# Gate and value weights by expert outputs: side by side fp32 products and a group sum in place of split products

## Chip, cores and metric

The kernel runs on one core of one Trainium2 chip. Its time is the device time of one execution in microseconds (us), and the median of several executions is what counts. Five engines work beside each other, each through its own instructions in order: TensorE (PE, with its weight loads listed apart as PEld), VectorE (DVE), ScalarE (ACT), GpSimd (POOL), and SyncE (SP), which issues the transfers.

## What is computed

Three layers follow one another; all inputs come as float64 and the output is float32.

```python
# chunked attention, 64 tokens a chunk, 8 heads of 64
attn = softmax(scale * q_c @ k_c.T); x = attn @ v_c            # x: 4608 x 512
# soft mixture of experts, 8 experts of 4 slots
logits = x @ phi                                               # 4608 x 32
slot_input = softmax(logits, axis=0).T @ x                     # 32 x 512
slot_out[e] = relu(slot_input[e] @ w1[e]) @ w2[e]              # 32 x 512
x2 = softmax(logits, axis=1) @ slot_out                        # 4608 x 512
# gated layer
g = x2 @ w_gate; val = x2 @ w_val                              # 512 -> 1536
out = (g * sigmoid(g) * val) @ w_out                           # 1536 -> 512
```

Since x2 has rank 32, the kernel never forms it. With C the 4608 x 32 matrix of combine weights, g = C @ (slot_out @ w_gate), and the same for val. The change lies in the small inner product slot_out @ w_gate and slot_out @ w_val.

## The kernel before

**Stages.** Attention, logits and slot inputs run until about 130 us, the experts until about 170 us, and the gated layer from there to the end. The rest concerns the gated layer.

**Chunks.** The 1536 inner columns come as six chunks `c` of 256 (`NSC`), so twelve tiles `f` of 128. Chunk 0 has a path of its own. For a chunk `c` of 1 to 5 the weights w_gate, w_val and w_out arrive as float64 words and are turned into float32 in halves `u` of 1024 words, in four steps over four turns of the main loop: `conv_a` (L174) takes the words apart on ACT and DVE, `conv_b` (L194) goes on with them, `conv_c` (L202) makes the exponent on DVE (L203) and multiplies on POOL (L216), and `conv_d` (L231) splits the float32 value into a high part, rounded to the short fp32r format by ACT (L237), and the rest, by POOL or DVE in turn (L242). High part and rest go into a tile `whl`. The queue `conv_q` goes through gate half 0, gate half 1, value 0, value 1, out 0, out 1 of each chunk; how far it is, `conv_pos()` (L262) counts.

**Inner product.** `emit_g` (L825) multiplies `so_hl` (slot_out transposed, in four blocks `kk` of 128 rows, its high part three times over and its rest once, in 128 columns) by the split weights: for gate and for value four blocks and two parts each, so 16 matmuls of 256 columns into the PSUM tile `gg_ps`. `evac_g` (L812) then copies them to `g_st` on ACT and replaces one group of 32 partitions by its rest on DVE. `try_g` (L958), at the end of a turn, calls it once the four gate and value halves have been through all four steps.

**Main loop** (L973). There are 108 pairs of a block `b` of 512 tokens and a tile `f`, in an order given by `SCHED`. Turn `n` issues in this order: `emit_gv` (L843), two matmuls `g_ps` and `v_ps`, then silu on ACT (L853) and the product `s_sb` on DVE (L854); `emit_hl` for the pair before (L870), its high part on ACT (L860) and its rest `lo_sb` on POOL (L867); one `conv_step`; `emit_out` (L877) for the pair two turns back, 12 matmuls of 512 columns (L894), and, when a group of pairs ends, the addition of four tiles of output to `part` (L912); and `try_g`. So each engine sees the turns in this order, and PE has 14 matmuls a turn beside the inner product.

**Buffers.** PSUM has three buffers for `g_ps`, `v_ps` and the inner product (`ps_g`). Weights, words and splits share 16 buffers (`wp`), which `freed` and `pump` hand on to the next transfer.

Of the kernel before, what the change touches and what calls it, by code (L numbers as in the profile page):

```python
# [8 lines left out]
F32 = mybir.dt.float32  # L9
F32R = mybir.dt.float32r  # L10
# [4 lines left out]
ACTF = mybir.ActivationFunctionType  # L15
ALU = mybir.AluOpType
# [18 lines left out]
def tile_attn_softmoe_swiglu(  # L35
# [12 lines left out]
    nc = tc.nc  # L48
# [6 lines left out]
    NSC = w_gate.shape[0]  # L55
# [10 lines left out]
    sel_big = const.tile([128, 4, 32], F32, name="sel_big")  # L66
# [10 lines left out]
    raw_t = {}  # L77
# [39 lines left out]

    hl_t = {}

    def alloc_hl(kind, c, pool):  # L120
        hl_t[kind, c] = wp.tile([128, 2048], F32R, tag="w", name="whl")

# [3 lines left out]
        tmp_t.append(pool.tile([128, 2048], I32, tag="w", name="tmp"))  # L126

    def sc_loads(c, kinds="gvo"):
        return [(f, kd, c) for kd in kinds for f in (load_raw, alloc_hl)]

    lq = [(load_gv0, 0), (alloc_tmp, 0)]
    EG = 4
# [27 lines left out]
    def freed(f, *a):  # L160
        slots[owner.pop((f.__name__, a))] += 1
        if auto[0]:
            pump()
# [37 lines left out]
    def conv_c():  # L201
        kind, c, u, hh, ex, m = stage["c"].pop(0)  # L202
        nc.vector.scalar_tensor_tensor(out=ex, in0=hh, scalar=0x8000, in1=ex,  # L203
                                       op0=ALU.bitwise_and, op1=ALU.bitwise_or)
        p = ex.bitcast(BF16)
        if c == 0 and kind != "o":
            nc.gpsimd.tensor_tensor(
                out=w_f32(u)[:, :, "gv".index(kind), :], in0=m.rearrange("p (k f) -> p k f", k=4),
                in1=p.rearrange("p (k f) -> p k f", k=4), op=ALU.mult,
            )  # L210
            if kind == "v":
                if u == 0:
                    freed(load_gv0, 0)
                freed(alloc_tmp, u)
            return
        nc.gpsimd.tensor_tensor(out=m, in0=m, in1=p, op=ALU.mult)  # L216
        stage["d"].append((kind, c, u, m))
        if u == 1:
            freed(load_raw, kind, c)
# [3 lines left out]
            return wf0  # L223
        return raw0[0, ff].bitcast(F32).rearrange("p (k a f) -> p k a f", a=2, f=128)

    def w_split(kind, c):
        return hl_t[kind, c].rearrange("p (k h f) -> p k h f", h=2, f=512 if kind == "o" else 256)

    n_d = [0]

    def conv_d(eng=None, hi_eng=None):  # L231
        kind, c, u, m = stage["d"].pop(0)
        k = 1 if kind == "o" else 2
        w = w_split(kind, c)[:, k * u:k * (u + 1)]
        m = m.rearrange("p (k f) -> p k f", k=k)
        if hi_eng is None:
            nc.scalar.activation(out=w[:, :, 0], in_=m, func=ACTF.Copy)  # L237
        else:
            hi_eng.tensor_copy(out=w[:, :, 0], in_=m)
        eng = eng or (nc.vector if n_d[0] % 2 else nc.gpsimd)  # L240
        n_d[0] += 1
        eng.tensor_tensor(out=w[:, :, 1], in0=m, in1=w[:, :, 0].bitcast(F32), op=ALU.subtract)  # L242

    def conv_ready():
        if not conv_q:
            return False
        kd, c, u = conv_q[-1]
        if c == 0 and kd != "o":
            return ("gv".index(kd), u) in raw0
        return (kd, c) in raw_t and (kd, c) in hl_t  # L250

    def conv_step(start=True, which="dcba"):
        for k, f in (("d", conv_d), ("c", conv_c), ("b", conv_b)):
# [8 lines left out]
    def conv_pos():  # L262
        n = len(conv_q) + sum(len(x) for x in stage.values())
        return 6 * NSC - n
# [6 lines left out]
    with tc.manual_schedule():  # L271
# [32 lines left out]
        for i in range(NV):  # L304
            nc.vector.memset(v_bd[i][0:64, 1], 0.0)
        nc.vector.tensor_reduce(
            out=sel_big[:, 0, :], in_=ident.rearrange("p (j s) -> p s j", s=32), axis=AX.X, op=ALU.add
        )
        nc.vector.tensor_tensor(
            out=sel_h.rearrange("p a s -> p (a s)"), in0=ident[:, 0:64], in1=ident[:, 64:128], op=ALU.add  # L310
# [237 lines left out]
        for k in range(NP + 1):  # L548
            a = k - 1
# [251 lines left out]
        ps_g = ctx.enter_context(tc.tile_pool(name="ps_g", bufs=3, space=PSUM, reuse_waits="tile"))  # L801
        ht2 = ctx.enter_context(tc.tile_pool(name="ht2", bufs=3, side="right"))
        g_st = ht2.tile([128, NSC, 2, 256], F32R, name="g_st", bufs=1)
        so_hl = ht2.tile([128, 4, 128], F32R, name="so_hl", bufs=1)

        def emit_so_hl():
            nc.scalar.activation(out=so_hl[:, :, 0:96], in_=so_t[:, :, 0:96], func=ACTF.Copy)
            nc.vector.tensor_tensor(
                out=so_hl[:, :, 96:128], in0=so_t[:, :, 0:32], in1=so_hl[:, :, 0:32].bitcast(F32), op=ALU.subtract
            )  # L810

        def evac_g(ps, gst):  # L812
            nc.scalar.activation(out=gst, in_=ps, func=ACTF.Copy)
# [8 lines left out]
                freed(load_gv0, ff)  # L822
            return lambda: evac_g(gp, g_st[:, 0, gi, ff * 128:(ff + 1) * 128])

        def emit_g(c):  # L825
            gp = ps_g.tile([128, 2, 256], F32, tag="g", name="gg_ps")
            for gi in range(2):
                w = w_split("gv"[gi], c)
                for kk in range(4):
                    for h in range(2):  # L830
                        nc.tensor.matmul(out=gp[:, gi], lhsT=so_hl[:, kk, :], rhs=w[:, kk, h],  # L831
                                         start=(kk == 0 and h == 0), stop=(kk == 3 and h == 1))
            evac_g(gp, g_st[:, c])
            freed(alloc_hl, "g", c)
            freed(alloc_hl, "v", c)

        hl = {}
        s_t = {}
# [38 lines left out]
        def emit_out(b, f, first, last, mid=None, subs=()):  # L877
            hi, lo = hl.pop((b, f))
            c, ff = f // 2, f % 2
            w = w_split("o", c)  # L880
            w_hi, w_lo = w[:, ff, 0], w[:, ff, 1]
            done = f == NFT - 1
            subs = dict(subs)
            if last and not done and b not in part:
                assert slots[0]
                slots[0] -= 1
                resv[0] -= 1
                part[b] = wp.tile([128, 4, DM], F32, tag="w", name="part"), True

            def product(t, i):  # L890
                x, w = ((hi, w_hi), (hi, w_lo), (lo, w_hi))[i]
                if first and i == 0:
                    acc_t[t] = ps_o.tile([128, DM], F32, tag="o", name=f"o{t}")
                nc.tensor.matmul(out=acc_t[t], lhsT=x[:, t * 128:(t + 1) * 128], rhs=w,  # L894
                                 start=(first and i == 0), stop=(last and i == 2))

            if mid:
                for i in range(3):
                    for t in range(4):
                        product(t, i)  # L900
                    if i == 0:
                        mid()
            for t in range(4):
                if not mid:
# [52 lines left out]

        def try_g():  # L958
            c = g_done[0]
            if c < NSC and conv_pos() >= 6 * c + 4:  # L960
                emit_g(c)
                g_done[0] += 1

        LAG = 2

# [7 lines left out]
        for n in range(1, len(seq) + LAG):  # L973
            if n < len(seq):
                c = gvs[n][1] // 2
                conv_until(6 * c + 4)
                while g_done[0] <= c:
                    try_g()
            if 1 < n < len(seq):
                emit_gv(*gvs[n])  # L980
            if 3 < n <= len(seq):
                emit_hl(*gvs[n - 1], nc.gpsimd)
            m = 1 if n == 2 else n - LAG if n > 3 else None
            start = 36 - len(conv_q) < RATE * n + R0
# [12 lines left out]
            if m is not None:
                out_step(m, subs)
                try_g()
            if n == 4:  # L1000
                emit_so_hl()


_INS = ['qk', 'v', 'moe_phi', 'moe_w1', 'moe_w2', 'moe2_w_gate', 'moe2_w_val', 'moe2_w_out']
# [48 lines left out]
```

## Time and profile before

| | us |
|---|---|
| median of 3 runs | 545.22 (544.48 to 545.23) |
| the profiled execution | 543.5 |
| its span in the trace | 541.7 |
| PE busy | 521.6 (96%) |
| DVE busy | 401.2 (74%) |
| ACT busy | 260.6 (48%) |
| POOL busy | 251.2 (46%) |

The span lies between the first and the last instruction; 1.8 us of the execution lie around it. A busy PE says only that matmuls were under way: they overlap, so that what one costs is read from start to start and not from its own duration.

### The profile page before, as it was taken

How to read it: one execution, taken by the hardware profiler on the slowest of the kernel's cores; microseconds unless marked ns; L12 is line 12 of the kernel's file. 1: busy time of each engine (PE TensorE's matmuls, PEld its weight loads, DVE VectorE, ACT ScalarE, POOL GpSimd, SP SyncE). 2: the span in 40 equal slices, each digit the busy share in tenths (PEclk: the TensorE clock that was granted, in tenths of full speed). 3: DMA queues.
4: the chain of work that ended last, by engine and by line, in shares of the span. 5: the costliest groups of instructions: out<-in, count | busy, mean ns of one | idle time of the engine just before them, and what ended most of it. 6: DMA issues, size and time to landing. Idle time of an engine off the chain costs nothing.

```text
span 541.7 us, 11050 instructions
## 1 busy us (share of the span) xinstructions
PE 521.6 (96%) x4389; PEld 409.0 (76%) x4389; DVE 401.2 (74%) x681; ACT 260.6 (48%) x505; POOL 251.2 (46%) x251
## 2 busy tenths in 40 slices
PE   7899999998999789999999999999999999999997
PEld 6788877873435568888888788788878888888885
DVE  5788888764765878898899978988888863444454
ACT  1344433333446666676555546555555543333331
POOL 3244343331003276675665646674666563443342
PEclk9999999999999999999999999999999999999999
DMA  8999999999999600102200240014000000222244
GB/s 326 405 363 400 353 400 342 412 415 379 422 416 413 267 1 16 64 1 79 77 1 0 79 155 2 4 74 156 0 1 0 2 1 1 77 79 89 103 179 173
DMA packets 23906, 91.09 MB, mean 168 GB/s; under 512 B 3120, under 2 KB 3120, under 8 KB 17968
## 3 DMA queue, kind: packets, MB, share of 16 engines
q1 hardware_dynamic: 23856, 90.40, 43.2%
q8 instruction: 34, 0.56, 0.4%
q14 instruction: 16, 0.13, 0.1%
HBM read 80.95 MB, written 9.44 MB: 167 GB/s over the span
## 4 chain that ended last, share of the span: by engine, by line
PE 87%; DVE 6%; ACT 2%; issue 2%; POOL 1%; DMA 1%; SPq 0%; ACTq 0%; DVEq 0%; POOLq 0%
PE o L894 52%; PE v_ps L850 4%; PE g_ps L850 4%; PE xa_ps L368 4%; PE s_ps L331 3%; PE so_ps L698 3%; PE xt_ps L404 3%; PE h_ps L655 3%; PE pt_ps L354 3%; PE gg_ps L831 2%; PE si_ps L487 2%; DVE m L339 1%; DVE ssb L341 1%; PE lt_ps L423 1%; PE xb_ps L368 1%
## 5 line engine op out<-in xcount | busy, mean ns | idle before, releaser
L894 PE MATMUL o<-whl,hi_sb 128*128 128x512 f32 x864 | 266.9, 390 | 2.8 <-ACT whl L237 2.6
L867 POOL TENSOR_TENSOR lo_sb<-s_sb,hi_sb 128x512 fp32r<-128x512 f32 x106 | 142.4, 1344 | 129.1 <-ACT hi_sb L860 127.2
L894 PEld LDWEIGHTS o<-whl,hi_sb 128*128 128x128 f32 x864 | 161.8, 188 | 37.6 <-ACT whl L237 3.0
L894 PE MATMUL o<-whl,lo_sb 128*128 128x512 f32 x432 | 168.8, 392 | 1.7 <-POOL lo_sb L867 1.6
L853 ACT ACTIVATE s_sb<-g_ps 128x512 f32<-128x512 f32 (+1 forms) x110 | 64.5, 589 | 133.9 <-PE g_ps L850 122.5
L854 DVE TENSOR_TENSOR s_sb<-s_sb,v_ps 128x512 f32<-128x512 f32 (+1 forms) x110 | 73.9, 674 | 68.5 <-ACT s_sb L853 65.3
L894 PEld LDWEIGHTS o<-whl,lo_sb 128*128 128x128 f32 x432 | 81.1, 188 | 21.4 <-POOL lo_sb L867 4.7
L860 ACT ACTIVATE hi_sb<-s_sb 128x512 fp32r<-128x512 f32 (+1 forms) x110 | 67.7, 617 | 2.4 <-DVE s_sb L854 2.4
L912 DVE TENSOR_TENSOR part<-part,o 128x512 f32<-128x512 f32 x100 | 62.0, 678 | 2.6 <-PE o L894 2.6
L321 POOL COPY vbd<-vbd 64x520 f32<-64x520 f32 x36 | 22.6, 628 | 70.0 <-DMA vbd<-in_v_dram 54.4
L216 POOL TENSOR_TENSOR mt<-mt,ex 128x512 f32<-128x512 f32 x32 | 38.3, 1196 | 30.8 <-DVE ex L203 22.0
L203 DVE SCALAR_TENSOR_TENSOR ex<-raw,ex 128x512 uint16<-128x512 uint16 x32 | 44.0, 1374 | 0.5 <-ACT ex L197 0.5
L850 PE MATMUL v_ps<-c_t,g_st 128*128 128x512 f32 (+1 forms) x110 | 42.4, 389 | 0.7 <-ACT s_sb L853 0.6
L850 PE MATMUL g_ps<-c_t,g_st 128*128 128x512 f32 (+1 forms) x110 | 42.2, 387 | 0.1
L356 ACT ACTIVATE pt<-pt_ps 128x512 f32<-128x512 f32 x36 | 19.5, 596 | 37.4 <-PE pt_ps L354 37.4
L198 DVE SCALAR_TENSOR_TENSOR mt<-mt,raw 128x512 f32<-128x512 f32 x32 | 34.6, 1081 | 0.1
L339 DVE TENSOR_REDUCE m<-s_ps 128x16 f32<-128x1024 f32 x18 | 22.1, 1225 | 14.7 <-PE s_ps L331 14.7
L368 PE MATMUL xa_ps<-vbd,pt 128*64 128x130 f32 x432 | 28.2, 277 | 0.5 <-issue 0.5
L190 DVE TENSOR_SCALAR mt<-raw 128x512 int32<-128x512 int32 x32 | 27.2, 851 | 0.0
L237 ACT ACTIVATE whl<-mt 128x512 fp32r<-128x512 f32 x32 | 20.3, 633 | 13.4 <-POOL mt L216 13.0
L368 PEld LDWEIGHTS xa_ps<-vbd,pt 128*64 128x64 f32 x432 | 23.7, 135 | 3.2 <-issue 2.3
L406 ACT ACTIVATE xt<-xt_ps 128x512 f32<-128x512 f32 (+1 forms) x36 | 19.3, 596 | 13.3 <-PE xt_ps L404 9.7
(131 smaller groups left out, 613.4 us busy)
## 6 DMA issues: line engine op xcount, KB each, us to landing
qk<-in_qk_dram SPq DMA_DIRECT2D x36, 512.0 KB, 6.4
w1t<-in_moe_w_dram SPq DMA_DIRECT2D x16, 1024.0 KB, 9.1
w2t<-in_moe_w_dram SPq DMA_DIRECT2D x15, 1024.0 KB, 13.5
vbd<-in_v_dram SPq DMA_DIRECT2D x36, 260.0 KB, 7.4
out_dram<-part SPq DMA_DIRECT2D x36, 256.0 KB, 2.1
raw<-in_moe_w_gate_dram SPq DMA_DIRECT2D x5, 1024.0 KB, 4.8
raw<-in_moe_w_val_dram SPq DMA_DIRECT2D x5, 1024.0 KB, 4.9
raw<-in_moe_w_out_dram SPq DMA_DIRECT2D x5, 1024.0 KB, 4.8
```

Source lines behind the costliest of these rows:

```text
L198: nc.vector.scalar_tensor_tensor(out=m, in0=m, scalar=-7.0, in1=lw.bitcast(F32), op0=ALU.add, op1=ALU.add)
L203: nc.vector.scalar_tensor_tensor(out=ex, in0=hh, scalar=0x8000, in1=ex, op0=ALU.bitwise_and, op1=ALU.bitwise_or)
L216: nc.gpsimd.tensor_tensor(out=m, in0=m, in1=p, op=ALU.mult)
L339: nc.vector.tensor_reduce(out=m, in_=sv, axis=AX.X, op=ALU.max)
L368: nc.tensor.matmul(out=banks[n // 3][64 * cc:64 * cc + 64, (n % 3) * 2 * VW:(n % 3 + 1) * 2 * VW], lhsT=pt_t[i][:, j, 64 * cc:64 * cc + 64 ...
L850: nc.tensor.matmul(out=ps[:, k], lhsT=g_st[:, c, gi, ff:ff + 128], rhs=c_blk(b)[:, k], start=True, stop=True)
L853: nc.scalar.activation(out=s[:, k], in_=gp[:, k], func=ACTF.Silu)
L854: nc.vector.tensor_tensor(out=s[:, k], in0=s[:, k], in1=vp[:, k], op=ALU.mult)
L860: nc.scalar.activation(out=hi[:, k], in_=s_t[b, f][:, k], func=ACTF.Copy)
L867: eng.tensor_tensor(out=lo[:, k], in0=s[:, k], in1=hi[:, k].bitcast(F32), op=ALU.subtract)
L894: nc.tensor.matmul(out=acc_t[t], lhsT=x[:, t * 128:(t + 1) * 128], rhs=w, start=(first and i == 0), stop=(last and i == 2))
L912: nc.vector.tensor_tensor(out=p[:, t], in0=p[:, t], in1=a, op=ALU.add)
```

## The change

The gate and value weights of chunks 1 to 5 are no longer split. `conv_c` writes its product into a float32 tile `gw`, four blocks of 128 rows by gate and value by 256 columns, and these halves are done there; `conv_d` is left for w_out alone. The inner product has two parts now, in two turns. `emit_ga` multiplies four blocks in float32, each by 32 columns of `so_t`, into four groups of 32 partitions of `ga_ps`, so that the sums over the blocks are not made yet. ACT makes the high part `ghi` of the whole, and DVE the rest `glo`. At the end of the next turn `emit_gb` multiplies each of the two by `sel_r`, a matrix of zeros and ones that adds the four groups and writes the sum three times (its last 32 columns are zero), and `evac_g` follows as before. `emit_sel` makes `sel_r` in place of `so_hl`.

```diff
+    def alloc_gw(c, pool):
+        gw_t[c] = pool.tile([128, 4, 2, 256], F32, tag="w", name="gw")
...
     def sc_loads(c, kinds="gvo"):
-        return [(f, kd, c) for kd in kinds for f in (load_raw, alloc_hl)]
+        gw = [(load_raw, kd, c) for kd in "gv"] + [(alloc_gw, c)]
+        return (gw if "g" in kinds else []) + [(load_raw, "o", c), (alloc_hl, "o", c)]
...
+        if kind != "o":
+            nc.gpsimd.tensor_tensor(
+                out=gw_t[c][:, 2 * u:2 * u + 2, "gv".index(kind)], in0=m.rearrange("p (k f) -> p k f", k=2),
+                in1=p.rearrange("p (k f) -> p k f", k=2), op=ALU.mult,
+            )
+            if u == 1:
+                freed(load_raw, kind, c)
+            return
         nc.gpsimd.tensor_tensor(out=m, in0=m, in1=p, op=ALU.mult)
         stage["d"].append((kind, c, u, m))
...
-        so_hl = ht2.tile([128, 4, 128], F32R, name="so_hl", bufs=1)
-
-        def emit_so_hl():
-            nc.scalar.activation(out=so_hl[:, :, 0:96], in_=so_t[:, :, 0:96], func=ACTF.Copy)
-            nc.vector.tensor_tensor(
-                out=so_hl[:, :, 96:128], in0=so_t[:, :, 0:32], in1=so_hl[:, :, 0:32].bitcast(F32), op=ALU.subtract
-            )
+        sel_r = ht2.tile([128, 128], F32R, name="sel_r", bufs=1)
+
+        def emit_sel():
+            nc.scalar.activation(out=sel_r[:, 0:96], in_=sel_big.rearrange("p j s -> p (j s)")[:, 0:96], func=ACTF.Copy)
+            nc.scalar.activation(out=sel_r[:, 96:128], in_=so_t[:, 0, 96:128], func=ACTF.Copy)
...
-        def emit_g(c):
-            gp = ps_g.tile([128, 2, 256], F32, tag="g", name="gg_ps")
-            for gi in range(2):
-                w = w_split("gv"[gi], c)
-                for kk in range(4):
-                    for h in range(2):
-                        nc.tensor.matmul(out=gp[:, gi], lhsT=so_hl[:, kk, :], rhs=w[:, kk, h],
-                                         start=(kk == 0 and h == 0), stop=(kk == 3 and h == 1))
+        gs_t = {}
+
+        def emit_ga(c):
+            gp = ps_g.tile([128, 512], F32, tag="g", name="ga_ps")
+            w = gw_t.pop(c)
+            for kk in range(4):
+                nc.tensor.matmul(out=gp[32 * kk:32 * kk + 32, :], lhsT=so_t[:, kk, 0:32],
+                                 rhs=w[:, kk].rearrange("p a f -> p (a f)"), start=True, stop=True,
+                                 tile_position=(0, 32 * kk))
+            hi = ht2.tile([128, 512], F32R, tag="ghi", name="ghi", bufs=1)
+            nc.scalar.activation(out=hi, in_=gp, func=ACTF.Copy)
+            lo = ht2.tile([128, 512], F32R, tag="glo", name="glo", bufs=1)
+            nc.vector.tensor_tensor(out=lo, in0=gp, in1=hi.bitcast(F32), op=ALU.subtract)
+            gs_t[c] = hi, lo
+            freed(alloc_gw, c)
+
+        def emit_gb(c):
+            gp = ps_g.tile([128, 2, 256], F32, tag="g", name="gb_ps")
+            for i, x in enumerate(gs_t.pop(c)):
+                nc.tensor.matmul(out=gp.rearrange("p a f -> p (a f)"), lhsT=sel_r, rhs=x, start=(i == 0), stop=(i == 1))
             evac_g(gp, g_st[:, c])
...
         def try_g():
             c = g_done[0]
-            if c < NSC and conv_pos() >= 6 * c + 4:
-                emit_g(c)
+            if c in gs_t:
+                emit_gb(c)
                 g_done[0] += 1
+            elif c < NSC and conv_pos() >= 6 * c + 4:
+                emit_ga(c)
```

**Where the instructions stand.** On PE, at chunk 1, the inner product of before (`gg_ps`, L831) follows the 12 output products of a turn:

```order
L850 MATMUL g_ps<-c_t,g_st 128x512
L850 MATMUL v_ps<-c_t,g_st 128x512
L894 MATMUL o_3211<-whl,hi_sb 128x512 x2
L894 MATMUL o_3211<-whl,lo_sb 128x512
L894 MATMUL o_3215<-whl,hi_sb 128x512 x2
L894 MATMUL o_3215<-whl,lo_sb 128x512
L894 MATMUL o_3219<-whl,hi_sb 128x512 x2
L894 MATMUL o_3219<-whl,lo_sb 128x512
L894 MATMUL o_3223<-whl,hi_sb 128x512 x2
L894 MATMUL o_3223<-whl,lo_sb 128x512
L831 MATMUL gg_ps<-whl,so_hl 128x256 x16
L850 MATMUL g_ps<-c_t,g_st 128x512
```

With the change the same piece begins with `ga_ps`, one turn earlier, ahead of the `g_ps` that is the first row above, and ends with the first of the two products `gb_ps` at the place where `gg_ps` stood:

```order
L841 MATMUL ga_ps<-gw,so_t 32x512 x4
L870 MATMUL g_ps<-c_t,g_st 128x512
L870 MATMUL v_ps<-c_t,g_st 128x512
L914 MATMUL o_3213<-whl,hi_sb 128x512 x2
L914 MATMUL o_3213<-whl,lo_sb 128x512
L914 MATMUL o_3217<-whl,hi_sb 128x512 x2
L914 MATMUL o_3217<-whl,lo_sb 128x512
L914 MATMUL o_3221<-whl,hi_sb 128x512 x2
L914 MATMUL o_3221<-whl,lo_sb 128x512
L914 MATMUL o_3225<-whl,hi_sb 128x512 x2
L914 MATMUL o_3225<-whl,lo_sb 128x512
L854 MATMUL gb_ps<-ghi,sel_r 128x512
```

So the four fp32 products moved one turn ahead and two products of 512 columns stand where the 16 of 256 columns were; chunks 2 to 5 are alike. With their waits (what engine's signal an instruction waits for stands in brackets), the rows of `ga_ps` are these:

```order
L841 MATMUL ga_ps<-gw,so_t 32x512 [waits DVE_49]
L841 MATMUL ga_ps<-gw,so_t 32x512
L841 MATMUL ga_ps<-gw,so_t 32x512 [waits Pool_49]
L841 MATMUL ga_ps<-gw,so_t 32x512
L870 MATMUL g_ps<-c_t,g_st 128x512 [waits Activation_49]
L870 MATMUL v_ps<-c_t,g_st 128x512 [waits DVE_49]
```

The third of the four, which reads half 1 of the weights, waits for POOL, and everything after it on PE stands behind that wait.

On POOL, at chunk 1 again, a value half went through its product (`mt<-mt,ex`, L216) in one turn, and through `conv_d` (`whl`, L242) a turn later for every other half; `lo_sb` is the rest of a pair, one a turn:

```order
L867 TENSOR_TENSOR lo_sb<-s_sb,hi_sb 128x512 x3
L216 TENSOR_TENSOR mt<-mt,ex 128x512
L867 TENSOR_TENSOR lo_sb<-s_sb,hi_sb 128x512
L242 TENSOR_TENSOR whl<-mt,whl 128x2x256
L867 TENSOR_TENSOR lo_sb<-s_sb,hi_sb 128x512
L216 TENSOR_TENSOR mt<-mt,ex 128x512
L867 TENSOR_TENSOR lo_sb<-s_sb,hi_sb 128x512 x3
```

With the change the products of value half 0 and value half 1 write `gw`, and no `whl` stands between the `lo_sb`:

```order
L887 TENSOR_TENSOR lo_sb<-s_sb,hi_sb 128x512 x3
L223 TENSOR_TENSOR gw<-mt,ex 128x2x256
L887 TENSOR_TENSOR lo_sb<-s_sb,hi_sb 128x512 x2
L223 TENSOR_TENSOR gw<-mt,ex 128x2x256
L887 TENSOR_TENSOR lo_sb<-s_sb,hi_sb 128x512 x3
```

The product of value half 1 (the second `gw`) keeps its turn, and stands behind the `lo_sb` of that turn. It is the one for which the third product `ga_ps` waits.

## Rows read from the trace of the kernel before

**Rows 1.** Stretch: length, busy PE, PEld, DVE, ACT, POOL, TensorE's clock, DMA share, GB/s

```profile
203.10:529.80 326.70, 326.64 (x1470) 269.77 (x1469) 246.25 (x333) 169.19 (x299) 184.79 (x142) 1.00 0.15 52
```

**Rows 2.** Chain that ended last: inner products of chunks 1 and 3 (start, us, what)

```profile
212.75 1.91 PE gg_ps L831 x16
...
318.95 1.91 PE gg_ps L831 x16
```

**Rows 3.** Timeline of PE about chunk 5's inner product (start, us, operation)

```profile
419.03 0.39 PE L850 MATMUL g_ps<-c_t,g_st 128*128 128x512 f32 x1
...
422.21 0.39 PE L850 MATMUL g_ps<-c_t,g_st 128*128 128x512 f32 x1
...
425.39 2.34 PE L831 MATMUL gg_ps<-whl,so_hl 128*128 128x256 f32 x16
427.56 0.40 PE L850 MATMUL g_ps<-c_t,g_st 128*128 128x512 f32 x1
```

**Rows 4.** Waits of PE's weight loads, 206 to 530 us (total, times, longest)

```profile
PEld o L894 <- POOL lo_sb L867: 1.7, 5, 0.4
PEld o L894 <- DVE part L912: 0.6, 2, 0.3
PEld gg_ps L831 <- DVE whl L242: 0.4, 2, 0.2
```

**Rows 5.** Timeline of DVE and POOL in the same turn as the first row of rows 3

```profile
420.15 0.69 DVE L854 TENSOR_TENSOR s_sb<-s_sb,v_ps 128x512 f32<-128x512 f32 x1 [0.77 <-ACT s_sb L853]
...
420.71 1.29 POOL L867 TENSOR_TENSOR lo_sb<-s_sb,hi_sb 128x512 fp32r<-128x512 f32 x1 [1.89 <-ACT hi_sb L860]
420.75 1.80 DVE L203 SCALAR_TENSOR_TENSOR ex<-raw,ex 128x512 uint16<-128x512 uint16 x1
...
422.63 1.17 POOL L216 TENSOR_TENSOR mt<-mt,ex 128x512 f32<-128x512 f32 x1 [0.62 <-PE g_ps L850]
```

**Rows 6.** Timeline of the same turn in chunk 2, from its g_ps on

```profile
258.96 0.39 PE L850 MATMUL g_ps<-c_t,g_st 128*128 128x512 f32 x1
...
260.68 0.72 DVE L203 SCALAR_TENSOR_TENSOR ex<-raw,ex 128x512 uint16<-128x512 uint16 x1
...
260.82 1.75 POOL L867 TENSOR_TENSOR lo_sb<-s_sb,hi_sb 128x512 fp32r<-128x512 f32 x1
...
262.52 1.18 POOL L216 TENSOR_TENSOR mt<-mt,ex 128x512 f32<-128x512 f32 x1
```

**Rows 7.** Timeline of PE: four fp32 products side by side (x8), and what follows

```profile
126.64 1.07 PE L487 MATMUL si_ps<-x_sb,e 128*32 128x512 f32 x8
127.64 0.33 PE L469 MATMUL e_ps<-ident,et 128*128 128x128 f32 x1
...
131.48 1.92 PE L655 MATMUL h_ps<-w1t,si_m 128*32 128x512 f32 x16 [0.34 <-DVE si_m L633]
133.34 0.38 PE L755 MATMUL zps<-za,sel_big 128*128 128x1 f32 x2
```

**Rows 8.** Groups by line, 203 to 450 us (count | busy us, mean ns | idle before)

```profile
L242 POOL TENSOR_TENSOR whl<-mt,whl 128x512 fp32r<-128x512 f32 x14 | 20.2, 1445 | 0.0
L237 ACT ACTIVATE whl<-mt 128x512 fp32r<-128x512 f32 x28 | 17.7, 633 | 8.5 <-POOL mt L216 8.2
L242 DVE TENSOR_TENSOR whl<-mt,whl 128x512 fp32r<-128x512 f32 x14 | 14.5, 1039 | 6.6 <-ACT whl L237 6.6
L814 DVE TENSOR_TENSOR g_st<-gg_ps,g_st 32x512 fp32r<-32x512 f32 x5 | 3.4, 690 | 6.0 <-ACT g_st L813 6.0
```

**Rows 9.** Timeline of two early turns: PE, POOL and the waits between them

```profile
193.34 1.34 POOL L242 TENSOR_TENSOR whl<-mt,whl 128x512 fp32r<-128x512 f32 x1
...
195.83 0.39 PE L850 MATMUL g_ps<-c_t,g_st 128*128 128x512 f32 x1
...
197.10 0.50 PE L894 MATMUL o<-whl,lo_sb 128*128 128x512 f32 x1 [0.20 <-POOL lo_sb L867]
...
203.07 0.39 PE L850 MATMUL g_ps<-c_t,g_st 128*128 128x512 f32 x1
```

More of the change, by code (lines that the diff above doesn't have):

```diff
@@ L118, in tile_attn_softmoe_swiglu @@
     hl_t = {}
+    gw_t = {}
+    def alloc_gw(c, pool):
+        gw_t[c] = pool.tile([128, 4, 2, 256], F32, tag="w", name="gw")
     def alloc_hl(kind, c, pool):
@@ L224, in w_f32, with w_split @@
         return raw0[0, ff].bitcast(F32).rearrange("p (k a f) -> p k a f", a=2, f=128)
-    def w_split(kind, c):
-        return hl_t[kind, c].rearrange("p (k h f) -> p k h f", h=2, f=512 if kind == "o" else 256)
+    def w_split(c):
+        return hl_t["o", c].rearrange("p (k h f) -> p k h f", h=2, f=512)
     n_d = [0]
@@ L232, in conv_d @@
         kind, c, u, m = stage["d"].pop(0)
-        k = 1 if kind == "o" else 2
-        w = w_split(kind, c)[:, k * u:k * (u + 1)]
-        m = m.rearrange("p (k f) -> p k f", k=k)
+        w = w_split(c)[:, u]
         if hi_eng is None:
-            nc.scalar.activation(out=w[:, :, 0], in_=m, func=ACTF.Copy)
+            nc.scalar.activation(out=w[:, 0], in_=m, func=ACTF.Copy)
         else:
-            hi_eng.tensor_copy(out=w[:, :, 0], in_=m)
+            hi_eng.tensor_copy(out=w[:, 0], in_=m)
         eng = eng or (nc.vector if n_d[0] % 2 else nc.gpsimd)
         n_d[0] += 1
-        eng.tensor_tensor(out=w[:, :, 1], in0=m, in1=w[:, :, 0].bitcast(F32), op=ALU.subtract)
+        eng.tensor_tensor(out=w[:, 1], in0=m, in1=w[:, 0].bitcast(F32), op=ALU.subtract)
     def conv_ready():
@@ L249, in conv_ready @@
             return ("gv".index(kd), u) in raw0
-        return (kd, c) in raw_t and (kd, c) in hl_t
+        return (kd, c) in raw_t and ((kd, c) in hl_t if kd == "o" else c in gw_t)
     def conv_step(start=True, which="dcba"):
@@ L823, in emit_g0 @@
             return lambda: evac_g(gp, g_st[:, 0, gi, ff * 128:(ff + 1) * 128])
-        def emit_g(c):
-            gp = ps_g.tile([128, 2, 256], F32, tag="g", name="gg_ps")
-            for gi in range(2):
-                w = w_split("gv"[gi], c)
-                for kk in range(4):
-                    for h in range(2):
-                        nc.tensor.matmul(out=gp[:, gi], lhsT=so_hl[:, kk, :], rhs=w[:, kk, h],
-                                         start=(kk == 0 and h == 0), stop=(kk == 3 and h == 1))
+        gs_t = {}
[16 more added lines that the diff above has]
+                nc.tensor.matmul(out=gp.rearrange("p a f -> p (a f)"), lhsT=sel_r, rhs=x, start=(i == 0), stop=(i == 1))
             evac_g(gp, g_st[:, c])
-            freed(alloc_hl, "g", c)
-            freed(alloc_hl, "v", c)
         hl = {}
@@ L879, in emit_out @@
             c, ff = f // 2, f % 2
-            w = w_split("o", c)
+            w = w_split(c)
             w_hi, w_lo = w[:, ff, 0], w[:, ff, 1]
@@ L1000, in tile_attn_softmoe_swiglu @@
             if n == 4:
-                emit_so_hl()
+                emit_sel()
 _INS = ['qk', 'v', 'moe_phi', 'moe_w1', 'moe_w2', 'moe2_w_gate', 'moe2_w_val', 'moe2_w_out']
```

## The prediction, made before the changed kernel was run

> **What bounds the kernel now.** I read first the busy time of the gated layer's main part [rows 1]: in 326.7 us PE is busy 326.64, with TensorE's clock at 1.00 of full speed (2.4 GHz), DVE 246, POOL 185, ACT 169. PE runs its instructions in order, so whatever is added to or taken from PE's own sequence here goes into the time, and a wait on PE is lost. What the other engines save is worth only what it takes away from PE's waits. Then the timeline of PE around an inner product [rows 3]: from one `g_ps` to the next a turn takes 422.21 - 419.03 = 3.18 us, 14 matmuls of 512 columns at 0.227. Then the inner product itself, from its start to the next `g_ps`: 1.91 us in three of five chunks, as the chain shows [rows 2], and 427.56 - 425.39 = 2.17 in the two that wait for DVE's `whl` on the way [rows 3, 4]. Sum of before: 3 x 1.91 + 2 x 2.17 = 10.1 us. Last the timeline of DVE and POOL in the turn that converts value half 1 [rows 5, 6], because the change asks for its result one turn sooner.
>
> **PE's own work.** Removed: the 10.1 us above. Added by `emit_gb`: 2 x 0.227 = 0.45 us a chunk. Added by `emit_ga`: four float32 products of 32 columns of weights and 512 moving columns. The trace has the same shape in the slot inputs and the experts [rows 7]: one set of four takes 127.64 - 126.64 = 1.00 us until the next ordinary matmul, two sets 133.34 - 131.48 = 1.86. So a set costs 0.86, and leaving it 0.14. Unhindered, a chunk would cost 1.00 + 0.45 = 1.45 in place of 2.02 on average, and the change would give 10.1 - 5 x 1.45 = 2.9 us.
>
> The entry into side by side mode, behind fp32r products, is in no row; the exit's 0.14 bounds it from the nearest row, nothing is the other end. I take nothing, because a longer wait follows that covers it. The Trainium skill, "TensorEngine Tiling (Array Packing)", Key Properties, says that changing the tiling mode drains TensorE. The trace agrees for the exit (0.14 us [rows 7]); by that rule the entry would cost about as much, some 0.7 us in five chunks where nothing else waits, and nothing in my sum.
>
> **The wait that the change adds.** Half 1 of value passes `conv_c` in the turn at whose end `ga_ps` stands, and the third of the four products waits for POOL's product of that same turn (the order of PE in the section on the change). Before, `gg_ps` came a turn later. In chunk 5, counted from that turn's `g_ps` at 419.03 [rows 3, 5]: `s_sb` on DVE starts at +1.12, since it needs the silu of that `g_ps`; L203 stands behind it on DVE, from +1.72 to +3.52; POOL's product runs from +3.60 to 422.63 + 1.17 - 419.03 = +4.77. PE reaches the place of `ga_ps` at +3.18. In chunk 2 [rows 6] the product ends at 262.52 + 1.18 - 258.96 = +4.74. The chain starts at a `g_ps` of PE itself, so a faster rest of the kernel doesn't shorten it: the same `g_ps` sets both sides. POOL's product cannot start before the `lo_sb` of its turn either, which is ahead of it in the queue.
>
> So PE waits 4.76 - 3.18 = 1.58 us, about 0.06 more to start again (a signal's way; my estimate, from L203's end at 422.55 and POOL's start at 422.63). Products one and two run in the wait. Products three and four, which go side by side, then take the set's whole 0.86 and the exit's 0.14. `ga_ps` costs 1.64 + 1.00 = 2.64, with `gb_ps` 3.09 a chunk, 15.5 us in all: **+5.4 us** against 10.1.
>
> Behind that wait stand PE's `g_ps` and `v_ps` and all that hangs on them. They are only late by the same time; the pairs in flight have their `lo_sb` ready earlier, so nothing is lost twice. `ghi` (0.6 us, as L813's copy of the same size; I take L237's 0.63 [rows 8]) and `glo` (0.69, as L814 [rows 8]) must end before `gb_ps`, a whole turn later: 0.2 + 0.63 + 0.69 is well under 3.18. Cost nothing while a turn stays over 2 us. The third buffer of `ps_g` goes to `ga_ps` and then to `gb_ps`, as it went to `gg_ps`, and each is free again after its DVE instruction; nothing.
>
> **What the other engines save.** Each chunk loses four L237 (0.63 on ACT) and four L242 (two on POOL at 1.45, two on DVE at 1.04 [rows 8]) and gains one `ghi` and one `glo`: ACT 1.9, POOL 2.9, DVE 1.4 us less. It counts where PE waits for them. Early, in two turns from 195.83 to 203.07 [rows 9], PE needs 7.24 us instead of 2 x 3.18: it waits for a `lo_sb` that stood behind a `whl` of 1.34 us on POOL, which goes: **-0.9**. Later, waits for `lo_sb` and `part` come to 1.7 + 0.6 = 2.3 us of idle weight loads in seven places [rows 4], some of it hidden. Some of these `lo_sb` are late behind a removed instruction, some behind POOL products that stay, so the bounds are nothing and -2.3; I take **-0.8**, a third, as several wait for ACT or DVE instead. `emit_sel` is two short ACT copies in place of one ACT and one DVE instruction, beside PE: nothing. Transfers: the same ones in the same order on SP, with five buffers a chunk instead of six, so none starts later: nothing. Attention and experts: untouched.
>
> **Sum.** +5.4 - 0.9 - 0.8 = +3.7 us. Against the profiled execution 543.5 + 3.7 = 547.2 (span 541.7 + 3.7 = 545.4); the median of the runs is 1.7 above that execution, so **548.9 us**. A measurement of this kernel can tell about 0.2%, 1.1 us, from no change.
>
> **Rivals.**
>
> *The product is there in time.* If PE never waited, the change would give 2.9, and the savings above 1.7: 545.2 - 4.6 = 540.6 us. It needs POOL's product to end within 3.18 us of the `g_ps`. Against it: silu, `s_sb`, L203 and the product stand one behind the other, and even with L203 at 0.72 as in chunk 2 they end at +3.7. Only if the order on DVE were another could it hold. Chance 0.08.
>
> *The wait shrinks and the savings are full.* L203 takes 1.80 us where it begins just after `lo_sb` on POOL [rows 5], and 0.72 where it begins first, when `lo_sb` takes 1.75 instead of 1.29 [rows 6]: one slows the other. If neither did, `lo_sb` would begin at +1.68 and end at +2.97, the product at about +4.2, and PE would wait 1.0: a chunk 2.5, +2.4 in all, less 0.9 + 2.3 is -0.8: 544.4 at the utmost, 545 to 546.5 for most of such cases. Chance 0.13. The Trainium skill, "GPSIMD Engine Reference", says in its table that GpSimd's SBUF interfaces are shared with VectorE, with contention by DVE instructions that have two SBUF inputs, as L203 has. The trace agrees, 1.80 against 0.72; the change takes nothing away from this pair.
>
> *The half set costs more.* Rows show sets of four only [rows 7]. If two products begun behind a wait ran one after the other, each chunk would pay 0.86 more: +4.3, 553 us. For it: no row of two. Against it: in a set the four begin within the same instant. Chance 0.06.
>
> **How the numbers follow.** Forecast 0.73, from 546.9 (savings in full) to 551.2 (no later saving, and waits longer by 0.3 in two chunks whose DVE is behind). Rivals 0.08, 0.13, 0.06. Faster by over 0.2%: the first rival and a little of the second, 0.10. Within 0.2%: most of the second, 0.10. Slower: 0.80. The range of 8 in 10 leaves out the first and third rival and reaches over the second: 544.9 to 551.2.
>
> **What would show it.** In the profile after: (1) `ga_ps` with a gap of about 1.6 us before its third product in each of five chunks, released by POOL's L223; (2) 2.6 us from its start to the next `g_ps`, 0.45 for `gb_ps` without a wait; (3) L223 ending 4.7 us after its turn's `g_ps`; (4) no wait for `lo_sb` in the turns near 196 and 200 us; (5) ACT, POOL and DVE less busy by about 9, 14 and 7 us. If PE shows no wait at `ga_ps`, the forecast is wrong in its main term; if the wait is there and the time is not up by 2 us or more, the savings were mis-sized.

## The result, and the profile after

The changed kernel takes **549.31 us** (median; 547.36 to 551.39) against 545.22: a ratio of 1.0068, interval 1.0040 to 1.0097. It is slower by 4.1 us, where 3.7 were forecast.

Part 1 of the page after (busy time, share of the span, instructions of each engine):

```profile
PE 526.7 (96%) x4359; PEld 404.2 (74%) x4359; DVE 403.7 (73%) x675; ACT 249.9 (45%) x491; POOL 235.8 (43%) x241
```

ACT and POOL are relieved by 10.7 and 15.4 us, DVE is not: it has 6 instructions less and is busy 2.5 us longer. PE, which bounds, has 30 matmuls less and is busy 5.1 us longer; that sum also holds the stretch at a lower clock that comes next.

The profiled execution took 551.39 us. Before the gated layer, about 128 to 134 us, TensorE's clock was at the lower of its two levels (1.2 instead of 2.4 GHz). From the set of four products shown here to the first `h_ps` product (at 135.50) it took 7.74 us, and 131.48 - 126.64 = 4.84 before [rows 7]: 2.9 of the 4.0 us by which the first `g_ps` comes later, at 177.64 instead of 173.61. The other 1.1 were there already at 127.76. Both lie ahead of the gated layer, and experiment 6, the same kernel, has its first `g_ps` at 174.00. These are that stretch (columns as in [rows 1]) and the set, 1.93 us where it took 1.07 before:

```profile
126.00:136.00 10.00, 8.91 (x63) 4.42 (x59) 4.04 (x19) 1.87 (x8) 1.74 (x6) 0.66 0.84 343
```

```profile
127.76 1.93 PE L499 MATMUL si_ps<-x_sb,e 128*32 128x512 f32 x8
```

So the kernels are compared within the gated layer: from the first `g_ps` to the start of the last matmul it takes 363.91 us before and 367.77 after, +3.9. For a finer account each turn, from one `g_ps` to the next, is held against the 3.173 us of an undisturbed one (the median turn of each profile). The account starts with the turn at 190.95 us before and at 195.00 after and ends with the last `g_ps`. The excess of its 102 turns sums to 14.55 us before and 18.38 after, **+3.8**.

The timeline of PE about chunk 5's inner product, which answers to [rows 3]:

```profile
425.92 0.39 PE L870 MATMUL g_ps<-c_t,g_st 128*128 128x512 f32 x1
...
428.87 0.39 PE L914 MATMUL o<-whl,lo_sb 128*128 128x512 f32 x1
429.18 1.05 PE L841 MATMUL ga_ps<-gw,so_t 128*32 128x512 f32 x4
430.73 1.05 PE L841 MATMUL ga_ps<-gw,so_t 128*32 128x512 f32 x4 [0.50 <-POOL gw L223]
431.71 0.50 PE L870 MATMUL g_ps<-c_t,g_st 128*128 128x512 f32 x1
432.05 0.39 PE L870 MATMUL v_ps<-c_t,g_st 128*128 128x512 f32 x1
...
435.02 0.39 PE L854 MATMUL gb_ps<-ghi,sel_r 128*128 128x512 f32 x1
435.25 0.39 PE L854 MATMUL gb_ps<-glo,sel_r 128*128 128x512 f32 x1
435.48 0.39 PE L870 MATMUL g_ps<-c_t,g_st 128*128 128x512 f32 x1
```

Each fp32 product has two records. The first two products start at 429.18, the other two only at 430.73, and the next `g_ps` at 431.71. The turn takes 431.71 - 425.92 = 5.79 us, 2.62 over an undisturbed one. The idle time that the row shows, 0.50, is not the price: before it PE is busy for 1.05 us with the first pair, which costs nothing of its own where all four products start together (experiments 1 and 2).

DVE and POOL in the same turn, which answers to [rows 5]:

```profile
427.04 0.69 DVE L874 TENSOR_TENSOR s_sb<-s_sb,v_ps 128x512 f32<-128x512 f32 x1 [0.77 <-ACT s_sb L873]
427.60 1.29 POOL L887 TENSOR_TENSOR lo_sb<-s_sb,hi_sb 128x512 fp32r<-128x512 f32 x1 [1.89 <-ACT hi_sb L880]
427.64 1.80 DVE L209 SCALAR_TENSOR_TENSOR ex<-raw,ex 128x512 uint16<-128x512 uint16 x1
429.52 1.16 POOL L223 TENSOR_TENSOR gw<-mt,ex 128x512 f32<-128x512 f32 x1 [0.63 <-DVE ex L209]
...
432.09 0.42 DVE L196 TENSOR_SCALAR mt<-raw 128x512 int32<-128x512 int32 x1
432.47 0.69 DVE L847 TENSOR_TENSOR glo<-ga_ps,ghi 128x512 fp32r<-128x512 f32 x1
```

POOL's product ends at 429.52 + 1.16 = 430.68, that is +4.76 after the turn's `g_ps`; the third product starts 0.05 later. `glo` ends at 433.16, well ahead of `gb_ps` at 435.02.

The waits of the gated layer (total, times, longest):

```profile
PEld ga_ps L841 <- POOL gw L223: 7.0, 5, 1.4
...
PEld o L914 <- POOL lo_sb L887: 2.6, 3, 1.8
...
PE ga_ps L841 <- POOL gw L223: 2.5, 5, 0.5
```

The new wait comes five times, once a chunk, and always for POOL's product. The weight loads' waits for `lo_sb`, eight of 4.7 us in all before, are three of 2.6. Before, over the whole gated layer, the line was:

```profile
PEld o L894 <- POOL lo_sb L867: 4.7, 8, 1.8
```

The early turns that stood in [rows 9] are now free of one:

```profile
197.47 0.50 PE L914 MATMUL o<-whl,lo_sb 128*128 128x512 f32 x1 [1.40 <-POOL lo_sb L887]
199.87 0.39 PE L870 MATMUL g_ps<-c_t,g_st 128*128 128x512 f32 x1
...
206.22 0.39 PE L870 MATMUL g_ps<-c_t,g_st 128*128 128x512 f32 x1
```

From 199.87 to 206.22 are 6.35 us, two undisturbed turns; the wait of 1.40 in the turn ahead, the first of the account, was there before as well (an excess of 1.70 now, 1.71 before).

### The profile page after: what moved, and what is told of

The parts are those of the page before. It is cut to its first block, busy times and chain, and to the rows that moved or that the text cites. A ratio compares the mean times of both kernels' runs of the same rounds, so it can differ in the third digit from the quotient of the medians.

```text
span 549.6 us, 10951 instructions
## 1 busy us (share of the span) xinstructions
PE 526.7 (96%) x4359; PEld 404.2 (74%) x4359; DVE 403.7 (73%) x675; ACT 249.9 (45%) x491; POOL 235.8 (43%) x241
## 5 line engine op out<-in xcount | busy, mean ns | idle before, releaser
L209 DVE SCALAR_TENSOR_TENSOR ex<-raw,ex 128x512 uint16<-128x512 uint16 x32 | 47.6, 1488 | 0.5 <-ACT ex L203 0.5
L204 DVE SCALAR_TENSOR_TENSOR mt<-mt,raw 128x512 f32<-128x512 f32 x32 | 39.1, 1221 | 0.1
L223 POOL TENSOR_TENSOR gw<-mt,ex 128x512 f32<-128x512 f32 x20 | 23.9, 1194 | 15.6 <-DVE ex L209 7.5
L870 PEld LDWEIGHTS g_ps<-c_t,g_st 128*128 128x128 f32 x110 | 20.6, 188 | 8.5 <-issue 4.2
L196 DVE TENSOR_SCALAR mt<-raw 128x512 int32<-128x512 int32 x32 | 26.2, 818 | 0.0
```

The lines of the kernel that those rows point to most:

```text
L196: nc.vector.tensor_scalar(out=mt, in0=hw, scalar1=0xFFFFF, scalar2=0x41000000, op0=ALU.bitwise_and, op1=ALU.bitwise_or)
L204: nc.vector.scalar_tensor_tensor(out=m, in0=m, scalar=-7.0, in1=lw.bitcast(F32), op0=ALU.add, op1=ALU.add)
L223: nc.gpsimd.tensor_tensor(out=gw_t[c][:, 2 * u:2 * u + 2, "gv".index(kind)], in0=m.rearrange("p (k f) -> p k f", k=2), in1=p.rearrange("p ...
L870: nc.tensor.matmul(out=ps[:, k], lhsT=g_st[:, c, gi, ff:ff + 128], rhs=c_blk(b)[:, k], start=True, stop=True)
```

## Experiments

**1. The first part one turn later.** `try_g` lets one turn go by before it calls `emit_ga`; all else stays.

```diff
+        due = set()
...
             elif c < NSC and conv_pos() >= 6 * c + 4:
-                emit_ga(c)
+                if c in due:
+                    emit_ga(c)
+                due.add(c)
```

> The changed kernel with both parts of the inner product one turn later: ga_ps two turns after value half 1 enters its last step instead of in the same turn, gb_ps one turn after that. Nothing is added or left out. Theory (the wait for POOL's product is the loss): the product ends 4.7 us after its turn's g_ps and PE is at ga_ps only after 6.4, so the wait goes; the turn with ga_ps takes 3.18 + about 0.1 (entry) + 1.0 + 0.1 = 4.4 us instead of 5.79, that with gb_ps 3.63 or a little more; five chunks save 5 x 1.4 to 1.55 = 7 to 7.8 us against the changed kernel, about 541 to 542 us, 3 to 4 us faster than before the change. Rival (the side by side set itself or its mode switches cost the time, and POOL is only named because it comes last): ga_ps still takes 2.6 us of PE, and the time stays within 1.5 us of the changed kernel.

Measured: 540.65 us (539.57 to 543.99), ratio 0.9908 [0.9877, 0.9938] to the kernel before: faster than both. The timeline of PE about chunk 5:

```profile
420.06 0.39 PE L870 MATMUL g_ps<-c_t,g_st 128*128 128x512 f32 x1
...
423.23 0.39 PE L870 MATMUL g_ps<-c_t,g_st 128*128 128x512 f32 x1
...
426.50 1.06 PE L841 MATMUL ga_ps<-gw,so_t 128*32 128x512 f32 x8
427.50 0.50 PE L870 MATMUL g_ps<-c_t,g_st 128*128 128x512 f32 x1
...
430.81 0.39 PE L854 MATMUL gb_ps<-ghi,sel_r 128*128 128x512 f32 x1
431.03 0.39 PE L854 MATMUL gb_ps<-glo,sel_r 128*128 128x512 f32 x1
431.26 0.39 PE L870 MATMUL g_ps<-c_t,g_st 128*128 128x512 f32 x1
```

and POOL's two instructions ahead of it:

```profile
421.74 1.29 POOL L887 TENSOR_TENSOR lo_sb<-s_sb,hi_sb 128x512 fp32r<-128x512 f32 x1 [1.89 <-ACT hi_sb L880]
423.66 1.17 POOL L223 TENSOR_TENSOR gw<-mt,ex 128x512 f32<-128x512 f32 x1 [0.63 <-PE g_ps L870]
```

The product ends at 424.83, again +4.77 after its own turn's `g_ps` at 420.06; but PE asks for it only at 426.50. All four products start together, in 1.00 us to the next `g_ps`, and the turn is 1.09 to 1.11 too long instead of 2.62. This is what the wait costs: 5 x 1.52 = 7.6 us, close to the 8.4 between the sums of the turns (18.4 and 10.0). Of the rest 0.74 lies in the first turn of the account, where no inner product stands (0.96 here, 1.70 in the changed kernel). That part is not the edit's: the changed kernel itself has 0.91 there in experiment 6. The turn in which `ga_ps` stands alone decides whether this change loses or gains.

**2. Without the late half.** The products of blocks 2 and 3 take blocks 0 and 1 again, at the place of the change.

```diff
-                                 rhs=w[:, kk].rearrange("p a f -> p (a f)"), start=True, stop=True,
+                                 rhs=w[:, kk % 2].rearrange("p a f -> p (a f)"), start=True, stop=True,
```

> The changed kernel with ga_ps at its old place, but its third and fourth product read the weights of blocks 0 and 1 again instead of 2 and 3; so half of the gate and value weights of chunks 1 to 5 is left out of the sum, with the same number and shape of matmuls. Theory (the wait for value half 1): half 0 passed its last step two or three turns earlier, so no wait is left at the same place, ga_ps takes 1.0 to 1.2 us from its start to the next g_ps, and the time is that of the kernel with ga_ps one turn later, 541 to 542 us. Rival (place or mode): ga_ps keeps 2.6 us, and the time stays at about 549. A third reading, that the place right after a group's last output products matters (PSUM or DVE busy with part), would leave some wait on DVE or ACT of 0.5 us or more.

Measured: 542.55 us (541.79 to 544.88), ratio 0.9949 [0.9926, 0.9972]. PE's timeline about chunk 5:

```profile
422.44 1.06 PE L841 MATMUL ga_ps<-gw,so_t 128*32 128x512 f32 x8
423.44 0.50 PE L870 MATMUL g_ps<-c_t,g_st 128*128 128x512 f32 x1
...
426.75 0.39 PE L854 MATMUL gb_ps<-ghi,sel_r 128*128 128x512 f32 x1
427.54 0.50 PE L854 MATMUL gb_ps<-glo,sel_r 128*128 128x512 f32 x1 [0.40 <-DVE glo L847]
427.88 0.40 PE L870 MATMUL g_ps<-c_t,g_st 128*128 128x512 f32 x1
```

The same instructions in the same place, without the one late operand: no wait, 1.00 us. So the wait belongs to half 1 of value and not to the place or to side by side products as such. What I had not foreseen is the second wait: in chunks 4 and 5 `gb_ps` stands for `glo`. DVE and POOL show why:

```profile
422.62 2.47 DVE L932 TENSOR_TENSOR part<-part,o 128x512 f32<-128x512 f32 x4
425.01 0.42 DVE L195 TENSOR_SCALAR ex<-raw 128x512 uint16<-128x512 uint16 x1
425.31 1.29 POOL L887 TENSOR_TENSOR lo_sb<-s_sb,hi_sb 128x512 fp32r<-128x512 f32 x1 [1.37 <-issue]
425.35 1.54 DVE L196 TENSOR_SCALAR mt<-raw 128x512 int32<-128x512 int32 x1
426.81 0.68 DVE L847 TENSOR_TENSOR glo<-ga_ps,ghi 128x512 fp32r<-128x512 f32 x1
```

In every chunk writes to `part` (four additions, in chunk 1 two copies) stand on DVE ahead of `glo`; in chunks 4 and 5 the next conversion, L195 and L196, stands there too. L196 takes 1.54 us, beginning just behind `lo_sb` on POOL; in the changed kernel the wait at `ga_ps` puts `lo_sb` off, L196 runs alone in 0.42 (432.09 in the rows above), and `glo` is early. The prediction's "well under 3.18" for `ghi` and `glo` counted their own times and no queue; it held in the changed kernel by the help of the wait. Each such wait costs 0.8 us with what follows it in the next turn, two of them 1.7: that is what this kernel takes more than experiment 1, 331.13 us against 329.47 from the second turn of the account to the last `g_ps`. (Both profiles show the clock lowered somewhere between 185 and 195 us, ahead of these turns.)

**3. The conversion ahead of the pair's products.** In each turn from n = 5 on the `conv_step` is issued before `emit_gv` and `emit_hl`, so that L209 and POOL's product don't stand behind `s_sb` and `lo_sb`. `ga_ps` stays in its place.

```diff
-            if 1 < n < len(seq):
-                emit_gv(*gvs[n])
-            if 3 < n <= len(seq):
-                emit_hl(*gvs[n - 1], nc.gpsimd)
+            def products():
+                if 1 < n < len(seq):
+                    emit_gv(*gvs[n])
+                if 3 < n <= len(seq):
+                    emit_hl(*gvs[n - 1], nc.gpsimd)
+            if n <= 4:
+                products()
...
+            if n > 4:
+                products()
```

> The changed kernel with the conversion step of each turn from n = 5 on put ahead of the turn's g_ps, silu, s_sb and lo_sb in program order instead of behind them. PE's order does not change. It tests the chain that sets the wait: L209 on DVE would no longer stand behind s_sb, which needs the same turn's g_ps, and POOL's product no longer behind lo_sb. If that queue order is the cause, the product of value half 1 ends before PE reaches ga_ps (3.2 us after g_ps), its wait is under 0.3 us and the five turns save about 7 us; but s_sb and lo_sb now stand behind up to 3 us of conversion on DVE and 1.2 on POOL, so PE may wait for lo_sb or v_ps buffers in other turns: net 541 to 548 us. If the chain is bound elsewhere (ACT's part of the conversion, or transfers), the wait of 1.5 us stays and the time is 549 or more.

Measured: 556.37 us (555.35 to 557.15), ratio 1.0195 [1.0153, 1.0236]. The wait at `ga_ps` is gone, 1.00 us in every chunk, and the time is worse than with it. The waits say where it went:

```profile
PEld o L914 <- POOL lo_sb L887: 18.9, 24, 1.7
...
PE o L914 <- POOL lo_sb L887: 9.6, 18, 1.2
```

A turn of it on ACT, DVE, POOL and PE:

```profile
419.94 0.62 ACT L880 ACTIVATE hi_sb<-s_sb 128x512 fp32r<-128x512 f32 x1
420.50 0.69 DVE L209 SCALAR_TENSOR_TENSOR ex<-raw,ex 128x512 uint16<-128x512 uint16 x1
421.27 1.16 POOL L223 TENSOR_TENSOR gw<-mt,ex 128x512 f32<-128x512 f32 x1 [2.50 <-DVE ex L209]
422.39 1.46 POOL L887 TENSOR_TENSOR lo_sb<-s_sb,hi_sb 128x512 fp32r<-128x512 f32 x1
423.90 0.50 PE L914 MATMUL o<-whl,lo_sb 128*128 128x512 f32 x1 [0.70 <-POOL lo_sb L887]
```

`hi_sb` is ready at 420.56, and before the move `lo_sb` would have started then. Now POOL has the product ahead of it, which waits for L209, and `lo_sb` ends only at 423.85. So the wait for POOL has moved to `lo_sb`, into 18 turns where the change waits in five. The net of 541 to 548 us that stood in the expectation was missed by the price of these turns.

**4. The removed splits put back as ballast.** The four halves of gate and value pass ACT and POOL or DVE once more, as before the change, into a tile that nothing reads.

```diff
...
+        if kind != "o":
+            x = dummy_t[0]
+            nc.scalar.activation(out=x[:, 0], in_=m, func=ACTF.Copy)
+            eng = nc.vector if n_d[0] % 2 else nc.gpsimd
+            n_d[0] += 1
+            eng.tensor_tensor(out=x[:, 1], in0=m, in1=x[:, 0].bitcast(F32), op=ALU.subtract)
+            return
```

> The changed kernel with the removed work on the other engines put back: each gate and value half of chunks 1 to 5 is split after its product as it was before the change (ACT copy, then POOL or DVE subtraction in turn), into a tile that nothing reads. PE and the place of ga_ps stay. It sizes what the removal of that work gave. My sum had 1.7 us (0.9 in the two early turns, 0.8 later); the traces before and after show 0.9 early and about 1.1 later. Theory: about 2 us slower than the changed kernel, with the waits for lo_sb near 196 and 200 us back, about 551 us on the same footing. Rival (that work never mattered to PE): within 0.5 us of the changed kernel in the gated layer.

Measured: 550.48 us (549.69 to 552.63), ratio 1.0092 [1.0060, 1.0123]. That is 0.9 to 2.4 thousandths above the two measurements of the changed kernel, 0.5 to 1.3 us, with overlapping intervals, so the medians alone don't settle the size; the turns do. PE's timeline of the early turns:

```profile
195.87 0.39 PE L880 MATMUL g_ps<-c_t,g_st 128*128 128x512 f32 x1
199.50 0.39 PE L880 MATMUL g_ps<-c_t,g_st 128*128 128x512 f32 x1
203.04 0.39 PE L880 MATMUL g_ps<-c_t,g_st 128*128 128x512 f32 x1
```

7.17 us for two turns, near the 7.24 before the change [rows 9], where the change has 6.35: 0.8 us are back. The later turns without an inner product have 1.37 in excess (0.60 in the change, 1.67 before), so another 0.8 is back. The waits at `ga_ps` in chunks 1 and 3 grow as well, by 0.3 and 0.2. From the second turn of the account to the last `g_ps` that makes 339.27 us against 337.15, 2.1 more, about the 2 that were expected. So the relief of the other engines is worth about 1.6 us to PE in turns without an inner product, and some 0.5 at the wait.

**5. Plain fp32 products.** At the place of experiment 1, four fp32 products with all 128 columns of `so_t`, summed in PSUM; `ghi`, `glo` and `gb_ps` go.

```diff
-                nc.tensor.matmul(out=gp[32 * kk:32 * kk + 32, :], lhsT=so_t[:, kk, 0:32],
-                                 rhs=w[:, kk].rearrange("p a f -> p (a f)"), start=True, stop=True,
-                                 tile_position=(0, 32 * kk))
...
+                nc.tensor.matmul(out=gp.rearrange("p a f -> p (a f)"), lhsT=so_t[:, kk, :],
+                                 rhs=w[:, kk].rearrange("p a f -> p (a f)"), start=(kk == 0), stop=(kk == 3))
```

> The kernel with ga_ps one turn later, but its four float32 products not side by side: each uses all 128 columns of so_t and they add up in one PSUM buffer, so that ghi, glo, sel_r's two products and the second turn go, and evac_g follows at once. It sizes what doing them side by side is worth. Theory (a side by side set of four costs as much as one product alone): in the trace of before eight float32 products of 128 columns took 1.9 us, 0.24 each, so one of 512 columns should take about 0.86 to 0.95 and four 3.4 to 3.8 us in place of the 1.0 + 0.1 + 0.14 + 0.45 = 1.7 us of the set with its group sum: 5 x 1.7 to 2.1 = 9 to 10 us slower than the kernel with ga_ps one turn later, about 550 us. Rival (the mode switches eat what the set gains): less than 3 us slower, under 544 us.

Measured: 550.81 us (549.76 to 551.66), ratio 1.0118 [1.0094, 1.0143]. PE's timeline about chunk 5:

```profile
432.26 3.60 PE L841 MATMUL ga_ps<-gw,so_t 128*128 128x512 f32 x8
435.29 0.80 PE L859 MATMUL g_ps<-c_t,g_st 128*128 128x512 f32 x1
435.92 0.39 PE L859 MATMUL v_ps<-c_t,g_st 128*128 128x512 f32 x1
```

435.29 - 432.26 = 3.03 us for the set, and `v_ps` comes 0.63 behind `g_ps` instead of 0.23: 3.4 us a chunk and no wait, where experiment 1 pays 1.1 + 0.6 = 1.7. In the turns that makes 9.2 us more than experiment 1, as expected. A plain product costs 3.43 / 4 = 0.86, as much as a whole set of four side by side [rows 7]. The eight records start 0.43 apart; side by side, four at a time start within 0.02 us, and the next four 0.45 later. So it is the side by side form that makes fp32 products pay here: without it even the better place loses.

**6. The changed kernel again**, beside experiment 5 on one chip.

> The changed kernel as it is, again, beside the one above on one chip: its profile was taken in an execution whose TensorE clock was at half for 6.8 us before the gated layer. Theory (that is no part of the change): a wait of 1.55 us at ga_ps in each of five chunks again, the gated layer from its first g_ps to its last matmul 367 to 369 us against 363.9 before, and a ratio to before of 1.005 to 1.009. Rival (the change itself slows the stages before the gated layer): the first g_ps comes 4 us later than before again, at 177 us or more, without a lowered clock.

Measured: 548.64 us (547.05 to 550.17), ratio 1.0083 [1.0060, 1.0106]; `ga_ps` 2.53 us to the next `g_ps` in all chunks, excess of the turn 2.62, of the next 0.60. The first `g_ps` is at 174.00, so the rival is out: the lower clock near 130 us is absent in this execution. It comes inside the gated layer instead (columns as in [rows 1]):

```profile
183.00:190.00 7.00, 6.54 (x15) 4.74 (x15) 4.44 (x9) 4.57 (x9) 1.28 (x1) 0.51 0.31 129
```

So the layer takes 369.24 us here, above the 367 to 369 that were expected. Behind that stretch, from the second turn of the account to the last `g_ps`, it is 337.25 us, against 337.15 in the first profile and 333.31 before: +3.9 and +3.8, with the clock at 1.00.

## Why the prediction was right, point by point

| term of the sum, us | forecast | measured in the turns |
|---|---|---|
| inner products before (turns' excess) | 10.1 | 10.3 |
| turn with `ga_ps`, a chunk | 2.64 | 2.62 |
| turn with `gb_ps`, a chunk | 0.45 | 0.60 |
| inner products after | 15.5 | 16.1 |
| early relief | -0.9 | -0.89 |
| later relief | -0.8 | -1.08 |
| sum | +3.7 | +3.8 |

The near agreement of the sum is in part luck: the inner products cost 0.4 more than forecast (+5.8 for +5.4) and the relief is 0.3 larger (-2.0 for -1.7), and the two nearly cancel.

**The wait** was right in cause and size. It was worked out from one turn of the kernel before: when POOL's product ends after the `g_ps` of its turn (+4.76 forecast, +4.76 found), against when PE comes to its place. Experiments 1 and 2 show the cause from two sides: a later place and an earlier operand both take the wait away, with the same four products in 1.00 us.

**Mis-sized: `gb_ps`.** Two products of 0.227 were counted, and the turn is 0.58 to 0.61 longer. 0.11 of the difference stands in the rows above: behind `ga_ps` the first `g_ps` is 0.34 ahead of `v_ps` instead of 0.23. The exit from the set was taken as over with the start of the next product. The prediction's price of a set's end, 0.14 [rows 7], lacked this second part, 0.55 us in five chunks; what the other 0.03 a chunk is stays open.

**The entry** into side by side mode, taken as hidden, is hidden: from 428.87 the next product would stand at 429.10, and the first pair starts at 429.18, so 0.09 us are there, ahead of a pair that ends before the wait does. In experiment 1, without a wait, the 0.09 are paid (426.18 + 0.23 to 426.50). The plain products of experiment 5 pay no entry: their first stands 0.23 behind the product ahead of it. The Trainium skill, "TensorEngine Tiling (Array Packing)", Key Properties, says that a change of the tiling mode drains TensorE. The trace agrees in that both changes cost time, 0.09 us at the entry, 0.14 and then 0.11 at the exit.

**The relief** came at the places named, the early part as forecast (-0.89), the later a little larger (-1.08 for -0.8, which was a third of a bound and a judgement). Experiment 4 takes 0.8 of each back.

**The range.** The bounds of the forecast, 546.9 and 551.2, are wider than the terms named for them give: savings in full make 545.2 + 5.4 - 0.9 - 2.3 = 547.4, and no later saving with two waits longer by 0.3 makes 545.2 + 5.4 - 0.9 + 0.6 = 550.3. The measured 549.31 lies inside either way.

**Point (5) of what would show it missed on DVE**: 7 us less were forecast, 2.5 more came. The removed L242 (16.3 to 6.5 us) and the added `glo` (3.5) make 6.3 less, but two groups that the change doesn't touch grew by 8.1; the rest is spread over small groups. The groups by line after, to be held against L203 and L198 before (44.0 and 34.6 us of the same counts):

```profile
L209 DVE SCALAR_TENSOR_TENSOR ex<-raw,ex 128x512 uint16<-128x512 uint16 x32 | 47.6, 1488 | 0.5 <-ACT ex L203 0.5
...
L204 DVE SCALAR_TENSOR_TENSOR mt<-mt,raw 128x512 f32<-128x512 f32 x32 | 39.1, 1221 | 0.1
```

Of these 64 instructions 45 take over 1 us, 40 before, and each of the long ones overlaps one of POOL. PE's waits for `lo_sb` became fewer all the same. L209 takes 1.80 us beside `lo_sb` and 0.69 in experiment 3 with POOL idle. The Trainium skill, "GPSIMD Engine Reference", Specifications, says that GpSimd shares its SBUF interfaces with VectorE, with contention from DVE instructions that have two SBUF inputs; the trace agrees.

**The rivals.** *The product is there in time*: not in the changed kernel, but experiment 1 makes it so, and its 540.65 us is the 540.6 worked out for this case. That the two agree so closely is luck: each chunk costs 1.69 instead of 1.45 (0.09 for the entry, 0.14 for the exit's second part), and against that stand a larger relief and the 0.74 of the first turn of the account, which is not the edit's. *The wait shrinks*: L209 takes 1.80 as before, nothing shrank. *The half set costs more*: 431.71 - 430.73 = 0.98 from the start of the late pair, as much as a set of four; a pair costs what a set costs, no more.

## What to carry to other kernels

Where a change lets a consumer be issued a step earlier, find in the old trace when its last operand ends, counted from an event that both hang on, and compare that with the consumer's new place on its engine: here 4.76 against 3.18 us, worth 7.6 us. If it is late, move the consumer back and not the producer ahead: one turn more on PE cost nothing that the turns show, and turned a loss of 0.7% into a gain of 0.9%, while the producer moved ahead put something more urgent behind it in 18 turns. Work taken off engines that don't bound gives only what PE had waited for, about 2 us here of some 26 on ACT and POOL.

## What I had not expected of the hardware

- The first product behind a stall or a change of mode takes longer: 0.34 us until the next one instead of 0.227, after the set (431.71 to 432.05), and behind plain waits (423.90 in experiment 3 to 424.24 for the next product; 427.54 to 427.88 in experiment 2).
- A pair of side by side fp32 products takes as long as four, 0.98 against 1.00 us to the next `g_ps`. Plain fp32 products of 128 columns take 3.03 us for four, and the one behind them loses another 0.40, so 0.86 each.
- TensorE's clock falls to its lower level for some microseconds in some executions of one kernel: in the changed kernel near 130 us in one profile, near 185 us in another (0.51 of full speed in the mean of 7 us each). Ahead of it PE had been idle for 1.02 and 0.76 us there and for 2.58 us here. The profile of the kernel before has all three gaps (1.02, 0.76 and 2.59 us) and kept its clock at 1.00, and so did the first profile of the changed kernel behind its third (2.60 us). So the gaps alone don't decide it; what does stays open. It cost 2.9 us in the one profile and 1.4 in the other (23.61 against 22.22 us from the first `g_ps` to the second turn of the account), a good part of what this change costs, so that one execution of each kernel could not have sized it.
- Whether the change makes the clock fall more often stays open too. In the executions beside experiment 6, on one chip, the mean clock is 0.996 to 0.999 in the kernel before and 0.994 to 0.996 in the changed one; beside experiments 1 to 4, on another chip, the kernel before alone goes from 0.991 to 0.999. The medians may hold some of this; the +3.8 of the turns holds none.
